# Retention and a gated feed-forward layer on one core: the state product padded to 128 rows, per-tile tables, and a new order of steps

## The chip, the cores and the metric

The kernel runs on one core of a Trainium2 chip. The metric is the device time of one execution in microseconds (us); a profiled execution gives the trace, whose span is a little shorter than that execution's time.

## The reference

Two layers follow each other. The first is a retention layer without softmax on `q`, `k`, `v` of shape (4, 8, 768, 64): batch, heads, tokens, head size.

```python
gamma = 1.0 - 2.0 ** (-5.0 - np.arange(H))
for t in range(S):
    state = gamma[None, :, None, None] * state + np.einsum('bhd,bhe->bhde', k[:, :, t], v[:, :, t])
    y[:, :, t] = scale * np.einsum('bhd,bhde->bhe', q[:, :, t], state)
```

Its result, 3072 tokens by 512, is the input `x` of the second layer, with weights of 512x1536, 512x1536 and 1536x512:

```python
gate = 1.0 / (1.0 + np.exp(-(x @ w_gate)))
val = x @ w_val
return (gate * val @ w_out).astype(np.float32)
```

All inputs and the output are float32; the kernel computes products in bfloat16 with float32 sums.

## The kernel before

**Tiles and pairs.** The 768 tokens are cut into six tiles t of 128 tokens. A pair P is one tile of two of the four batch elements, so P = 2t and 2t + 1 make a tile of all four: 512 columns of the second layer's input `xT`. Twelve pairs in all; tile t's feed-forward part runs while tile t + 1's retention part is prepared.

**Retention in chunks.** For a pair, q and k are transposed into `qkT` (two heads of 64 above each other on 128 partitions), by TensorE for pairs 0 to 3 (step T) and by DMA transposes that SyncE (SP) issues for the later ones (step J). `scores` multiplies k and q of a head (64 rows), `masks` multiplies the scores by a decay table on VectorE into `st`, `intra` multiplies v and `st` (128x64 stationary) into y, and before it `inter` adds the part of the earlier tiles: the running state times q, 64x64 per head, heads in two halves of the array. `state` multiplies the scaled k (`kt`) and v into the bank `z`, `state_sum` adds it to `za` on VectorE, and `state_out` scales `za` to the next tile's first token into `zq`, by ScalarE in four slices. `y_out` evicts y into `xT` on VectorE, times a table `taby`. The kernel keeps k scaled by gamma to the minus token, so one mask `maskd` (made from row 0 of `tabk`) and one `taby`, both relative to the tile, serve all tiles after the first.

**Feed-forward.** An up step (`up`, 128 of the 1536 hidden columns; `up_half` works on two such blocks and half of the tokens) makes four matmuls of 512 columns for the gate and four for the value into two banks, a sigmoid on ScalarE and a product on VectorE into `hT`. Tile 0 goes down by plain products (`down`). Tiles 1 to 5 use a seven-product scheme (`product` 1 to 7 of six matmuls of 256 columns, for two halves X and Y of the rows), with sums of hidden blocks on VectorE (`hidden_sums`, step S) and sums of weight blocks on GpSimd (POOL) with two casts on ScalarE (`weight_sums`, step W). `fast_out` evicts products 5, 6, 7 and 4 and stores finished rows from SP.

**Order.** Every engine runs its instructions in the order of the program. After a written prologue the program order is one string of steps per tile, `ORDER`; a minus sign means the tile before. Steps: u is `up`, a and b the two halves of `up_half`, d `down`, S and W the sums, X and Y products, L loads of a pair's k, q and v issued by POOL, H a tiny POOL copy that holds POOL until a pair's transposes have landed, J and T the transposes, k (VectorE) and m, n (ScalarE, four heads each) the scaling of k, O `state_out`, F the block of a new pair alone, E of a done pair alone, B of both.

```python
        "u1 u2 k0 u3 k1 u4 Z0 u5 u6 Z1 u7 u8 J4 J5 k2 T2 u9 F2 u10 u11",
```

A block in B runs inter (done), scores (new), intra (done), state (new) on TensorE, and y_out (done), masks (new), state_sum (new) on VectorE. All of PSUM's banks but one (the `z` bank) form one pool of seven that steps take in turn; a step waits until its bank has been read by its last reader.

**Transfers.** k, q, v and the weights come through POOL's queue (256 KB each for a pair's k, q and v); output rows and the DMA transposes are issued by SP.

Of the kernel before, what the change touches and what calls it, by code (L numbers as in the profile page):

```python
# [9 lines left out]
F32 = mybir.dt.float32  # L10
BF16 = mybir.dt.bfloat16
I32 = mybir.dt.int32
AX = mybir.ActivationFunctionType
ALU = mybir.AluOpType
# [3 lines left out]
def kernel(  # L18
# [10 lines left out]
    nc = tc.nc  # L29
    B, H, S, D = q.shape  # L30
    N_TOK, D_MODEL = out.shape
    D_FF = moe_w_gate.shape[1]
    C = 128
    NT = S // C
# [25 lines left out]
    def load(P, *what):  # L60
        for n in what:
            held, x = {"k": (kn, k), "q": (qn, q), "v": (vn, v)}[n]
            held[P] = ld.tile([C, 2 * H, D], BF16, tag=n, name=n + "n")
            nc.gpsimd.dma_start(out=held[P], in_=src(x, P))  # L64

    def load_one(P, c, *what):
        for n in what:
            held, x = {"k": (kn, k), "q": (qn, q), "v": (vn, v)}[n]
            if P not in held:
                held[P] = ld.tile([C, 2 * H, D], BF16, tag=n, name=n + "n")  # L70
            t, j = divmod(P, 2)
            nc.gpsimd.dma_start(out=heads(held[P], c),
                                in_=x[2 * j + c, :, t * C:(t + 1) * C, :].rearrange("h s d -> s h d"))
# [53 lines left out]
    for h in range(H):  # L127
        nc.scalar.activation(mask0[:, h % 2, h // 2, :], dist, AX.Exp, scale=lg[h], bias=lsc)
    maskd = const.tile([128, 2, NP, C], F32, name="maskd")
    tabk = const.tile([128, NT, H], F32, name="tabk")  # L130
    tabz = const.tile([128, NT, NP], F32, name="tabz")
    taby = const.tile([128, NP, C], F32, name="taby")

# [6 lines left out]
    def table_y():  # L140
        for p in range(NP):
            nc.scalar.activation(taby[:, p, :], toky, AX.Exp, scale=lgp[:, p:p + 1], bias=lsc)

    def table_mask():
        for i in range(2):
            nc.gpsimd.affine_select(maskd[:, i], tabk[:, 0, i:H:2].unsqueeze(2).to_broadcast([128, NP, C]),
                                    pattern=[[0, NP], [1, C]], base=0, channel_multiplier=-1,
                                    compare_op=ALU.is_ge, fill=0.0)

    qkT, kt, sc, st, y, zz, za, zq, xT = {}, {}, {}, {}, {}, {}, {}, {}, {}

# [22 lines left out]

    def scaled(P, part):
        x = kn[P].rearrange("s (c h) d -> s c h d", c=2)
        if part in (None, 0):
            kt[P] = ld.tile([C, 2 * H, D], BF16, tag="kt", name="kt", bufs=2)  # L180
        to = kt[P].rearrange("s (c h) d -> s c h d", c=2)
        if part is None:
            nc.vector.tensor_tensor(to, x, tabk[:, P // 2, :].unsqueeze(1).unsqueeze(3).to_broadcast([C, 2, H, D]),
                                    op=ALU.mult)
            return
        for h in range(part * NP, (part + 1) * NP):
            nc.scalar.activation(to[:, :, h, :], x[:, :, h, :], AX.Copy, scale=tabk[:, P // 2, h:h + 1])  # L187
# [9 lines left out]
    def masks(P, c):  # L197
        st[P, c] = []
        for i in range(2):
            s = at.tile([128, NP, C], BF16, tag="st", name="st", bufs=8)  # L200
            nc.vector.tensor_tensor(s, sc[P, c][i], (mask0 if P < 2 else maskd)[:, i], op=ALU.mult)  # L201
            st[P, c].append(s)

    def inter(P, c):
        y[P, c] = bank([128, NP, C])
        if P > 1:
            for p in range(NP):
                for i in range(2):
                    half = slice(i * D, (i + 1) * D)
                    nc.tensor.matmul(y[P, c][half, p, :], zq[P % 2][half, c, p, :], qkT[P][half, 1, c, p, :],  # L210
                                     start=(p == 0), stop=False, skip_group_check=True)
# [7 lines left out]
    def y_out(P, c, eng="a"):  # L219
        t = P // 2  # L220
        if t not in xT:
            xT[t] = at.tile([128, NP, 512], BF16, tag="xT", name="xT")
        col = (P % 2 * 2 + c) * C
        o = xT[t][:, :, col:col + C]
        if t == 0:
            (nc.scalar.copy if eng == "a" else nc.vector.tensor_copy)(o, y[P, c])  # L226
        else:
            nc.vector.tensor_tensor(o, y[P, c], taby, op=ALU.mult)  # L228

# [16 lines left out]
    def state_out(P):  # L246
        j = P % 2
        zq[j] = at.tile([128, 2, NP, D], BF16, tag=f"zq{j}", name="zq", bufs=1)
        for p in range(NP):
            nc.scalar.activation(zq[j][:, :, p, :], za[j][:, :, p, :], AX.Copy,  # L250
                                 scale=tabz[:, P // 2 + 1, p:p + 1])

    def has_state(P):
        return P is not None and P < NPAIR - 2

    def block(done, new):
        if done is not None:
            for c in range(2):
                inter(done, c)
        if new is not None:  # L260
            for c in range(2):
                scores(new, c)
        if done is not None:
            for c in range(2):
                intra(done, c)
        if has_state(new):
            state(new)
        if done is not None:
            for c in range(2):
                y_out(done, c)  # L270
        if new is not None:
            for c in range(2):
                masks(new, c)
        if has_state(new):
            state_sum(new)
# [4 lines left out]

    def up(t, n1, lo=0, hi=512):
        if t not in hT:
            hT[t] = ffn.tile([128, NFF, 512], BF16, tag="hT", name="hT", bufs=2)
        ps = []
        for w in (wg, wv):
            u = bank([128, 512])
            for kk in range(KT):
                nc.tensor.matmul(u[:, lo:hi], w[:, kk, n1 * 128:(n1 + 1) * 128], xT[t][:, kk, lo:hi],  # L288
                                 start=(kk == 0), stop=(kk == KT - 1))
            ps.append(u)  # L290
        gs = ffn.tile([128, 512], F32, tag="gs", name="gs")
        nc.scalar.activation(gs[:, lo:hi], ps[0][:, lo:hi], AX.Sigmoid)  # L292
        nc.vector.tensor_tensor(hT[t][:, n1, lo:hi], gs[:, lo:hi], ps[1][:, lo:hi], op=ALU.mult)  # L293

# [19 lines left out]
    def weight_sums(g, eng):  # L314
        fs = slice(2 * g, 2 * g + 2)
        b11, b12 = (wo2[:, fs, 0, c:c + 256] for c in (0, 256))
        b21, b22 = (wo2[:, fs, 1, c:c + 256] for c in (0, 256))
        t3 = ffn.tile([128, 2, 256], F32, tag="t3", name="t3", bufs=2)
        t2 = ffn.tile([128, 2, 256], F32, tag="t2", name="t2", bufs=2)
        eng.tensor_tensor(wt[:, 0, fs], b12, b11, op=ALU.subtract)  # L320
# [45 lines left out]
    def fast_out(t, i, n):  # L366
# [13 lines left out]
        if n == 7:  # L380
            nc.vector.tensor_tensor(hi[:, 256:], p5, a[:, :256], op=ALU.add)  # L381
        if n == 4:
            nc.scalar.copy(hi[:, :256], a[:, :256])
            nc.sync.dma_start(out=out[rows[1], :], in_=hi)

# [54 lines left out]
    transposes(1, 0, [0, 1], "a")  # L440
    table_y()
    keep_on(6)
    transposes(1, 1, [0, 1], "v", "v")
    scores(1, 0)
    scores(1, 1)
# [9 lines left out]
    for s in range(3, NFF // 2):  # L455
        load_gate_val(s)
    table_mask()
    load(2, "k", "q", "v")
    load(3, "k", "q", "v")
    for s in range(4):  # L460
        load_out(s)
    load(4, "k", "q", "v")
    load(5, "k", "q", "v")

    STEPS = {
        "u": lambda t, n: up(t, n),
        "a": lambda t, n: up_half(t, n, 0),
        "b": lambda t, n: up_half(t, n, 1),
# [8 lines left out]
        "T": lambda t, P: (new_qkT(P), transposes(P, 0, [0, 1], "a"), transposes(P, 1, [0, 1], "a")),  # L477
        "k": lambda t, P: scaled(P, None),
        "m": lambda t, P: scaled(P, 0),
# [3 lines left out]
        "B": lambda t, P: block(P - 1, P if P < NPAIR else None),  # L483
        "F": lambda t, P: block(None, P),
        "E": lambda t, P: block(P, None),
    }
    ORDER = [
        "u1 u2 k0 u3 k1 u4 Z0 u5 u6 Z1 u7 u8 J4 J5 k2 T2 u9 F2 u10 u11",
        "E2 k3 T3 a0 a2 F3 a4 a6 E3 O2 a8 W0 b0 O3 b2 W1 b4 b6 W2 m4 n4 a10 b8 H5 L6 L7 F4 b10 m5 -d0 n5 "
        "-d1 -d2 B5 J6 O4 -d3 S0 -d4 -d5 E5 J7 O5 -d6 S1 -d7 S2",  # L490
        "u0 -X1 -X2 u1 -X5 m6 u2 n6 -X3 -X6 u3 -X7 H7 L8 L9 u4 S0 -X4 F6 u5 m7 -Y1 -Y2 u6 n7 -Y5 u7 J8 "
        "-Y3 -Y6 u8 S1 J9 -Y7 u9 -Y4 B7 O6 u10 u11 E7 O7 S2",
        "-X1 -X2 u0 -X5 m8 u1 n8 -X3 -X6 u2 -X7 H9 L10 L11 u3 -X4 F8 u4 S0 m9 -Y1 -Y2 u5 n9 -Y5 u6 J10 "
        "-Y3 -Y6 u7 J11 -Y7 u8 S1 -Y4 B9 O8 u9 u10 E9 O9 u11 S2",
        "-X1 -X2 u0 -X5 u1 -X3 -X6 u2 -X7 u3 -X4 F10 u4 S0 -Y1 -Y2 u5 -Y5 u6 -Y3 -Y6 u7 -Y7 u8 S1 -Y4 B11 "
        "u9 u10 E11 u11 S2",
# [42 lines left out]
```

## Time and profile before

| | |
|---|---|
| time, median of three runs | 230.87 us (230.03 to 230.97) |
| the profiled execution's own time | 230.49 us |
| its span | 228.8 us |
| TensorE (PE) busy | 214.9 us, 94% |
| VectorE (DVE) busy | 139.8 us, 61% |
| ScalarE (ACT) busy | 102.8 us, 45% |
| GpSimd (POOL) busy | 70.4 us, 31% |
| moved by DMA | 25.22 MB, mean 110 GB/s |
| granted TensorE clock, mean | 0.989 |

In the page's slice lines a digit is the busy share of one of 40 slices of the span, in tenths (9 is 90% or more); a slice is 5.72 us. A timeline row gives the start, the time from the first start to the last end, the engine, the line of the kernel, the operation with output and inputs, the number of instructions merged into the row, and in brackets the idle time before it and what ended it. TensorE's matmuls are pipelined and their ends are modelled, so rows that follow each other overlap by some 0.16 us; and a few of its records are missing, which leaves a hole of one matmul in a row of otherwise even starts.

### The profile page before, as it was taken

How to read it: one execution, taken by the hardware profiler on the slowest of the kernel's cores; microseconds unless marked ns; L12 is line 12 of the kernel's file. 1: busy time of each engine (PE TensorE's matmuls, PEld its weight loads, DVE VectorE, ACT ScalarE, POOL GpSimd, SP SyncE). 2: the span in 40 equal slices, each digit the busy share in tenths (PEclk: the TensorE clock that was granted, in tenths of full speed). 3: DMA queues.
4: the chain of work that ended last, by engine and by line, in shares of the span. 5: the costliest groups of instructions: out<-in, count | busy, mean ns of one | idle time of the engine just before them, and what ended most of it. 6: DMA issues, size and time to landing. Idle time of an engine off the chain costs nothing.

```text
span 228.8 us, 4813 instructions
## 1 busy us (share of the span) xinstructions
PE 214.9 (94%) x1933; PEld 138.6 (61%) x1958; DVE 139.8 (61%) x266; ACT 102.8 (45%) x237; POOL 70.4 (31%) x77
## 2 busy tenths in 40 slices
PE   6668998999999999999999999999999999999992
PEld 6554444688885556566556565566566566664682
DVE  4763756876454973675693774983764974435630
ACT  7492465427776327273447362443233223323231
POOL 8978955699638001900092000000000000000000
PEclk9799999999999999999999999999999999999998
DMA  9999999999949999999999965200201101111013
GB/s 129 143 175 196 196 164 158 204 171 140 150 74 132 174 142 199 129 175 161 182 79 155 161 71 116 70 0 12 83 0 46 49 1 46 49 46 46 3 46 140
DMA packets 103703, 25.22 MB, mean 110 GB/s; under 512 B 93952, under 2 KB 100608, under 8 KB 103680
## 3 DMA queue, kind: packets, MB, share of 16 engines
q0 software_dynamic: 81248, 13.90, 79.7%
q1 hardware_dynamic: 22432, 11.01, 23.8%
q8 instruction: 15, 0.25, 0.5%
q14 instruction: 8, 0.07, 0.1%
HBM read 28.31 MB, written 6.29 MB: 151 GB/s over the span
## 4 chain that ended last, share of the span: by engine, by line
PE 77%; DMA 9%; POOL 6%; DVE 5%; issue 1%; ACT 0%; POOLq 0%; DVEq 0%
PE ff L288 36%; PE ff L363 19%; PE ff L304 9%; DMA qn<-in_q_dram 5%; PE ff L405 4%; DMA wv<-in_moe_w_val_dram 4%; PE ff L194 2%; PE ff L210 2%; PE ff L216 2%; DVE xT L228 2%; PE z L235 1%; DVE st L201 1%; POOL vn L64 1%; POOL kn L64 1%; POOL wg L85 1%
## 5 line engine op out<-in xcount | busy, mean ns | idle before, releaser
L293 DVE TENSOR_TENSOR hT<-gs,ff 128x512 bf16<-128x512 f32 (+1 forms) x61 | 41.1, 678 | 47.0 <-PE ff L288 39.6
L292 ACT ACTIVATE gs<-ff 128x512 f32<-128x512 f32 (+1 forms) x61 | 35.8, 589 | 63.5 <-PE ff L288 56.1
L288 PE MATMUL ff<-xT,wg 128*128 128x512 bf16 (+1 forms) x227 | 59.7, 376 | 2.9 <-DVE xT L226 1.1
L288 PE MATMUL ff<-xT,wv 128*128 128x512 bf16 (+1 forms) x239 | 61.2, 375 | 0.5
L288 PEld LDWEIGHTS <-wv 128*128 128x128 bf16 x244 | 23.9, 98 | 27.9
L288 PEld LDWEIGHTS <-wg 128*128 128x128 bf16 x244 | 22.7, 98 | 21.5 <-DVE xT L226 1.3
L363 PEld LDWEIGHTS <-hT 128*128 128x128 bf16 x240 | 23.4, 98 | 8.6 <-issue 1.0
L201 DVE TENSOR_TENSOR st<-ff,maskd 128x512 bf16<-128x512 f32 x40 | 24.8, 682 | 0.5 <-PE ff L194 0.4
L363 PEld LDWEIGHTS <-hs 128*128 128x128 bf16 x180 | 17.6, 98 | 5.4 <-issue 0.2
L363 PE MATMUL ff<-wt,hT 128*128 128x256 bf16 x120 | 16.0, 272 | 0.5 <-DVE ob L381 0.3
L363 PE MATMUL ff<-wt,hs 128*128 128x256 bf16 x120 | 16.2, 273 | 0.0
L228 DVE TENSOR_TENSOR xT<-ff,taby 128x512 bf16<-128x512 f32 x20 | 12.8, 684 | 5.2 <-PE ff L216 5.2
L250 ACT ACTIVATE zq<-za,tabz 128x128 bf16<-128x128 f32 x40 | 12.8, 390 | 6.6 <-PE ff L210 3.3
L187 ACT ACTIVATE kt<-kn,tabk 128x128 bf16<-128x128 bf16 x48 | 15.0, 390 | 0.0
L363 PE MATMUL ff<-wo,hT 128*128 128x256 bf16 x120 | 14.6, 273 | 0.1
L64 POOL DMA_DIRECT2D vn<-in_v_dram x12 | 14.0, 1169 | 1.7 <-DMA qn<-in_q_dram 0.6
L309 DVE TENSOR_TENSOR hT<-gs,ff 128x512 bf16<-128x512 f32 x12 | 8.1, 686 | 10.2 <-PE ff L304 7.3
L64 POOL DMA_DIRECT2D kn<-in_k_dram x11 | 12.8, 1165 | 2.7 <-DMA vn<-in_v_dram 1.3
L64 POOL DMA_DIRECT2D qn<-in_q_dram x11 | 12.7, 1158 | 1.4 <-PE ff L165 0.8
L304 PE MATMUL ff<-xT,wg 128*128 128x256 bf16 x96 | 12.5, 273 | 0.2 <-DVE xT L228 0.2
L304 PE MATMUL ff<-xT,wv 128*128 128x256 bf16 x96 | 12.4, 273 | 0.0
L417 POOL COPY kept<-qkT 128x2 bf16<-128x2 bf16 x3 | 0.6, 187 | 37.9 <-DMA qkT<-qn 37.9
(72 smaller groups left out, 242.5 us busy)
## 6 DMA issues: line engine op xcount, KB each, us to landing
out_dram<-ob SPq DMA_DIRECT2D x24, 256.0 KB, 2.3
vn<-in_v_dram POOLq DMA_DIRECT2D x12, 256.0 KB, 10.5
kn<-in_k_dram POOLq DMA_DIRECT2D x11, 256.0 KB, 8.1
qn<-in_q_dram POOLq DMA_DIRECT2D x11, 256.0 KB, 11.6
wo<-in_moe_w_out_dram POOLq DMA_DIRECT2D x4, 384.0 KB, 13.7
wg<-in_moe_w_gate_dram POOLq DMA_DIRECT2D x5, 256.0 KB, 9.2
wv<-in_moe_w_val_dram POOLq DMA_DIRECT2D x5, 256.0 KB, 9.1
raw<-in_k_dram SPq DMA_DIRECT2D x1, 256.0 KB, 3.4
```

The lines of the kernel that those rows point to most:

```text
L64: nc.gpsimd.dma_start(out=held[P], in_=src(x, P))
L187: nc.scalar.activation(to[:, :, h, :], x[:, :, h, :], AX.Copy, scale=tabk[:, P // 2, h:h + 1])
L201: nc.vector.tensor_tensor(s, sc[P, c][i], (mask0 if P < 2 else maskd)[:, i], op=ALU.mult)
L228: nc.vector.tensor_tensor(o, y[P, c], taby, op=ALU.mult)
L250: nc.scalar.activation(zq[j][:, :, p, :], za[j][:, :, p, :], AX.Copy, scale=tabz[:, P // 2 + 1, p:p + 1])
L288: nc.tensor.matmul(u[:, lo:hi], w[:, kk, n1 * 128:(n1 + 1) * 128], xT[t][:, kk, lo:hi], start=(kk == 0), stop=(kk == KT - 1))
L292: nc.scalar.activation(gs[:, lo:hi], ps[0][:, lo:hi], AX.Sigmoid)
L293: nc.vector.tensor_tensor(hT[t][:, n1, lo:hi], gs[:, lo:hi], ps[1][:, lo:hi], op=ALU.mult)
L304: nc.tensor.matmul(u[:, i], w[:, kk, (n1 + i) * 128:(n1 + i + 1) * 128], xT[t][:, kk, lo:lo + 256], start=(kk == 0), stop=(kk == KT - 1))
L309: nc.vector.tensor_tensor(hT[t][:, n1:n1 + 2, lo:lo + 256], gs, ps[1], op=ALU.mult)
L363: nc.tensor.matmul(to, left, right, start=(f == 0 and n in (1, 2)), stop=(f == NFF // 2 - 1), skip_group_check=True)
L405: nc.tensor.matmul(o, hT[t][:, n1, sm * 128:(sm + 1) * 128], wo[:, n1, :], start=(n1 == 0), stop=(n1 == NFF - 1))
```

## The change

- `inter` takes its stationary from `zbd`, one bfloat16 tile per pair of the tile with zeros off the diagonal blocks: 128 rows by 64 columns, and q of both heads as the moving side. The zeros are written once, by two memsets.
- `state_out` is two plain casts of `za`, one per half of the partitions. The decay that it applied moves into the tables: every tile has its own `maskd` and `taby`, made by POOL in `tile_tables` (step G, two affine selects and one product), tile 1's behind the loads of pairs 2 and 3, the others between the weight sums and between loads.
- A block runs scores (new), inter (done), intra (done), state (new), and on VectorE masks, y_out, state_sum.
- T2 stands behind u9, and F2 (as f, without its sum) behind u10; step p11 is u11 without its product, and that product (h) and the sum (V) follow E2. S1 stands before u8 or directly behind product 7. The slices n of the scaled k stand behind evictions.
- The table of y in the prologue stands behind the transposes of pair 1. k and q tiles have four buffers instead of five, t2 and t3 one instead of two.
- In the last tile the second row block of each half is stored in two halves, the very last half from ScalarE's queue.

The diff, shortened to its changed lines:

```diff
@@ -60,14 +60,14 @@
             held, x = {"k": (kn, k), "q": (qn, q), "v": (vn, v)}[n]
-            held[P] = ld.tile([C, 2 * H, D], BF16, tag=n, name=n + "n")
+            held[P] = ld.tile([C, 2 * H, D], BF16, tag=n, name=n + "n", bufs=5 if n == "v" else 4)
             nc.gpsimd.dma_start(out=held[P], in_=src(x, P))
...
             if P not in held:
-                held[P] = ld.tile([C, 2 * H, D], BF16, tag=n, name=n + "n")
+                held[P] = ld.tile([C, 2 * H, D], BF16, tag=n, name=n + "n", bufs=5 if n == "v" else 4)
             t, j = divmod(P, 2)
@@ -126,10 +126,13 @@
         nc.scalar.activation(mask0[:, h % 2, h // 2, :], dist, AX.Exp, scale=lg[h], bias=lsc)
-    maskd = const.tile([128, 2, NP, C], F32, name="maskd")
+    zbd = [const.tile([128, 2, NP, C], BF16, name=f"zbd{i}") for i in range(2)]
+    for z in zbd:
+        nc.vector.memset(z, 0.0)
     tabk = const.tile([128, NT, H], F32, name="tabk")
     tabz = const.tile([128, NT, NP], F32, name="tabz")
-    taby = const.tile([128, NP, C], F32, name="taby")
+    taby0 = const.tile([128, NP, C], F32, name="taby0")
+    maskd, taby = {}, {}
@@ -139,17 +142,20 @@
         for p in range(NP):
-            nc.scalar.activation(taby[:, p, :], toky, AX.Exp, scale=lgp[:, p:p + 1], bias=lsc)
-
-    def table_mask():
+            nc.scalar.activation(taby0[:, p, :], toky, AX.Exp, scale=lgp[:, p:p + 1], bias=lsc)
+
+    def tile_tables(t):
+        maskd[t] = at.tile([128, 2, NP, C], F32, tag="maskd", name="maskd")
         for i in range(2):
-            nc.gpsimd.affine_select(maskd[:, i], tabk[:, 0, i:H:2].unsqueeze(2).to_broadcast([128, NP, C]),
+            nc.gpsimd.affine_select(maskd[t][:, i], tabk[:, t, i:H:2].unsqueeze(2).to_broadcast([128, NP, C]),
                                     pattern=[[0, NP], [1, C]], base=0, channel_multiplier=-1,
                                     compare_op=ALU.is_ge, fill=0.0)
-
-
-
-    qkT, kt, sc, st, y, zz, za, zq, xT = {}, {}, {}, {}, {}, {}, {}, {}, {}
+        taby[t] = at.tile([128, NP, C], F32, tag="taby", name="taby")
+        nc.gpsimd.tensor_tensor(taby[t], taby0, tabz[:, t, :].unsqueeze(2).to_broadcast([128, NP, C]), op=ALU.mult)
+
+
+
+    qkT, kt, sc, st, y, zz, za, xT = {}, {}, {}, {}, {}, {}, {}, {}
@@ -174,14 +180,14 @@
-    def scaled(P, part):
+    def scaled(P, part, eng=None):
         x = kn[P].rearrange("s (c h) d -> s c h d", c=2)
...
         if part is None:
-            nc.vector.tensor_tensor(to, x, tabk[:, P // 2, :].unsqueeze(1).unsqueeze(3).to_broadcast([C, 2, H, D]),
-                                    op=ALU.mult)
+            eng.tensor_tensor(to, x, tabk[:, P // 2, :].unsqueeze(1).unsqueeze(3).to_broadcast([C, 2, H, D]),
+                              op=ALU.mult)
             return
@@ -198,7 +204,7 @@
             s = at.tile([128, NP, C], BF16, tag="st", name="st", bufs=8)
-            nc.vector.tensor_tensor(s, sc[P, c][i], (mask0 if P < 2 else maskd)[:, i], op=ALU.mult)
+            nc.vector.tensor_tensor(s, sc[P, c][i], (mask0 if P < 2 else maskd[P // 2])[:, i], op=ALU.mult)
             st[P, c].append(s)
@@ -207,7 +213,7 @@
                     half = slice(i * D, (i + 1) * D)
-                    nc.tensor.matmul(y[P, c][half, p, :], zq[P % 2][half, c, p, :], qkT[P][half, 1, c, p, :],
+                    nc.tensor.matmul(y[P, c][half, p, :], zbd[P % 2][:, c, p, half], qkT[P][:, 1, c, p, :],
                                      start=(p == 0), stop=False, skip_group_check=True)
@@ -225,7 +231,7 @@
         else:
-            nc.vector.tensor_tensor(o, y[P, c], taby, op=ALU.mult)
+            nc.vector.tensor_tensor(o, y[P, c], taby[t], op=ALU.mult)
@@ -245,40 +251,40 @@
         j = P % 2
-        zq[j] = at.tile([128, 2, NP, D], BF16, tag=f"zq{j}", name="zq", bufs=1)
-        for p in range(NP):
-            nc.scalar.activation(zq[j][:, :, p, :], za[j][:, :, p, :], AX.Copy,
-                                 scale=tabz[:, P // 2 + 1, p:p + 1])
+        for i in range(2):
+            half = slice(i * D, (i + 1) * D)
+            nc.scalar.copy(zbd[j][half, :, :, half], za[j][half])
...
-    def block(done, new):
-        if done is not None:
-            for c in range(2):
-                inter(done, c)
+    def block(done, new, sum_now=True):
         if new is not None:
...
             for c in range(2):
+                inter(done, c)
+            for c in range(2):
                 intra(done, c)
...
             state(new)
+        if new is not None:
+            for c in range(2):
+                masks(new, c)
         if done is not None:
...
                 y_out(done, c)
-        if new is not None:
-            for c in range(2):
-                masks(new, c)
-        if has_state(new):
+        if has_state(new) and sum_now:
             state_sum(new)
...
-    def up(t, n1, lo=0, hi=512):
+    gated = {}
+
+    def up(t, n1, lo=0, hi=512, finish=True):
         if t not in hT:
@@ -290,7 +296,13 @@
         nc.scalar.activation(gs[:, lo:hi], ps[0][:, lo:hi], AX.Sigmoid)
-        nc.vector.tensor_tensor(hT[t][:, n1, lo:hi], gs[:, lo:hi], ps[1][:, lo:hi], op=ALU.mult)
+        gated[t, n1] = (hT[t][:, n1, lo:hi], gs[:, lo:hi], ps[1][:, lo:hi])
+        if finish:
+            up_finish(t, n1)
+
+    def up_finish(t, n1):
+        to, gs, val = gated.pop((t, n1))
+        nc.vector.tensor_tensor(to, gs, val, op=ALU.mult)
@@ -315,8 +327,8 @@
         b21, b22 = (wo2[:, fs, 1, c:c + 256] for c in (0, 256))
-        t3 = ffn.tile([128, 2, 256], F32, tag="t3", name="t3", bufs=2)
-        t2 = ffn.tile([128, 2, 256], F32, tag="t2", name="t2", bufs=2)
+        t3 = ffn.tile([128, 2, 256], F32, tag="t3", name="t3", bufs=1)
+        t2 = ffn.tile([128, 2, 256], F32, tag="t2", name="t2", bufs=1)
         eng.tensor_tensor(wt[:, 0, fs], b12, b11, op=ALU.subtract)
@@ -379,9 +391,14 @@
             nc.vector.tensor_tensor(hi[:, 256:], p5, a[:, :256], op=ALU.add)
+            if t == NT - 1:
+                nc.sync.dma_start(out=out[rows[1], 256:], in_=hi[:, 256:])
         if n == 4:
             nc.scalar.copy(hi[:, :256], a[:, :256])
-            nc.sync.dma_start(out=out[rows[1], :], in_=hi)
+            if t == NT - 1:
+                (nc.scalar if i else nc.sync).dma_start(out=out[rows[1], :256], in_=hi[:, :256])
+            else:
+                nc.sync.dma_start(out=out[rows[1], :], in_=hi)
@@ -438,9 +455,9 @@
     transposes(1, 0, [0, 1], "a")
-    table_y()
     keep_on(6)
     transposes(1, 1, [0, 1], "v", "v")
+    table_y()
     scores(1, 0)
@@ -454,9 +471,9 @@
         load_gate_val(s)
-    table_mask()
     load(2, "k", "q", "v")
     load(3, "k", "q", "v")
+    tile_tables(1)
     for s in range(4):
@@ -464,6 +481,8 @@
         "u": lambda t, n: up(t, n),
+        "p": lambda t, n: up(t, n, finish=False),
+        "h": lambda t, n: up_finish(t, n),
         "a": lambda t, n: up_half(t, n, 0),
@@ -475,24 +494,28 @@
         "T": lambda t, P: (new_qkT(P), transposes(P, 0, [0, 1], "a"), transposes(P, 1, [0, 1], "a")),
-        "k": lambda t, P: scaled(P, None),
+        "G": lambda t, g: tile_tables(g),
+        "k": lambda t, P: scaled(P, None, nc.vector),
+        "K": lambda t, P: scaled(P, None, nc.gpsimd),
         "m": lambda t, P: scaled(P, 0),
...
         "F": lambda t, P: block(None, P),
+        "f": lambda t, P: block(None, P, False),
+        "V": lambda t, P: state_sum(P),
         "E": lambda t, P: block(P, None),
...
     ORDER = [
-        "u1 u2 k0 u3 k1 u4 Z0 u5 u6 Z1 u7 u8 J4 J5 k2 T2 u9 F2 u10 u11",
-        "E2 k3 T3 a0 a2 F3 a4 a6 E3 O2 a8 W0 b0 O3 b2 W1 b4 b6 W2 m4 n4 a10 b8 H5 L6 L7 F4 b10 m5 -d0 n5 "
-        "-d1 -d2 B5 J6 O4 -d3 S0 -d4 -d5 E5 J7 O5 -d6 S1 -d7 S2",
-        "u0 -X1 -X2 u1 -X5 m6 u2 n6 -X3 -X6 u3 -X7 H7 L8 L9 u4 S0 -X4 F6 u5 m7 -Y1 -Y2 u6 n7 -Y5 u7 J8 "
-        "-Y3 -Y6 u8 S1 J9 -Y7 u9 -Y4 B7 O6 u10 u11 E7 O7 S2",
-        "-X1 -X2 u0 -X5 m8 u1 n8 -X3 -X6 u2 -X7 H9 L10 L11 u3 -X4 F8 u4 S0 m9 -Y1 -Y2 u5 n9 -Y5 u6 J10 "
-        "-Y3 -Y6 u7 J11 -Y7 u8 S1 -Y4 B9 O8 u9 u10 E9 O9 u11 S2",
-        "-X1 -X2 u0 -X5 u1 -X3 -X6 u2 -X7 u3 -X4 F10 u4 S0 -Y1 -Y2 u5 -Y5 u6 -Y3 -Y6 u7 -Y7 u8 S1 -Y4 B11 "
+        "u1 u2 k0 u3 k1 u4 Z0 u5 u6 Z1 u7 u8 J4 J5 k2 u9 T2 u10 f2 p11",
+        "E2 -h11 V2 k3 T3 a0 a2 F3 a4 a6 E3 O2 a8 W0 b0 O3 G2 b2 W1 b4 m4 b6 W2 G3 n4 a10 b8 H5 L6 L7 F4 "
+        "m5 b10 n5 -d0 -d1 -d2 B5 J6 O4 -d3 S0 -d4 -d5 E5 J7 O5 -d6 S1 -d7 S2",
+        "u0 -X1 -X2 u1 -X5 m6 u2 -X3 -X6 n6 u3 -X7 H7 L8 G4 L9 u4 S0 -X4 F6 u5 m7 -Y1 -Y2 u6 -Y5 n7 u7 J8 "
+        "-Y3 -Y6 S1 u8 J9 -Y7 u9 -Y4 B7 O6 u10 u11 E7 O7 S2",
+        "-X1 -X2 u0 -X5 m8 u1 -X3 -X6 n8 u2 -X7 H9 L10 G5 L11 u3 -X4 F8 u4 S0 m9 -Y1 -Y2 u5 -Y5 n9 u6 J10 "
+        "-Y3 -Y6 u7 J11 -Y7 S1 u8 -Y4 B9 O8 u9 u10 E9 O9 u11 S2",
+        "-X1 -X2 u0 -X5 u1 -X3 -X6 u2 -X7 u3 -X4 F10 u4 S0 -Y1 -Y2 u5 -Y5 u6 -Y3 -Y6 u7 -Y7 S1 u8 -Y4 B11 "
         "u9 u10 E11 u11 S2",
```

## The prediction

> **What bounds the kernel now.** I read the page's busy times and slices first.
>
> ```profile
> PE 214.9 (94%) x1933; PEld 138.6 (61%) x1958; DVE 139.8 (61%) x266; ACT 102.8 (45%) x237; POOL 70.4 (31%) x77
> PE   6668998999999999999999999999999999999992
> DMA  9999999999949999999999965200201101111013
> ```
>
> TensorE (PE) is full from the fourth slice (17 us) to the last; up to there VectorE and ScalarE hand work to each other. DMA is full until slice 23 (131 us), so a load in that time lands when the queue gets to it, not when it is issued. What remains to be saved is what a PE-bound stretch loses between matmuls. The timeline of PE alone shows it, start to start, first at places without a named wait:
>
> ```profile
> 143.00 0.63 PE L210 MATMUL ff<-qkT,zq 64*64 64x128 bf16 x16
> 143.56 0.62 PE L194 MATMUL ff<-qkT 64*128 64x128 bf16 x16
> 144.11 0.64 PE L216 MATMUL ff<-st,vn 128*64 128x128 bf16 x16
> 144.58 0.42 PE L235 MATMUL z<-vn,kt 128*64 128x64 bf16 x16
> 144.93 1.04 PE L288 MATMUL ff<-xT,wg 128*128 128x512 bf16 x3
> ...
> 148.49 0.63 PE L210 MATMUL ff<-qkT,zq 64*64 64x128 bf16 x16
> 149.06 0.64 PE L216 MATMUL ff<-st,vn 128*64 128x128 bf16 x16
> ```
>
> Inter (L210) to scores (L194) is 0.56 us, scores to intra (L216) 0.55, but intra to state (L235), both 128*64, only 0.47 for the same 16 matmuls of 128 columns. Inter to intra in the lone block is 0.57. So a change of the array's shape (64*64, 64*128, 128*64) costs 0.09 to 0.10 us, and a group without one takes 0.47. Then the places with a wait, in the same timeline:
>
> ```profile
> 33.59 0.61 PE L165 MATMUL ff<-ident,kn 128*128 128x128 bf16 x8
> 35.16 0.62 PE L165 MATMUL ff<-ident,qn 128*128 128x128 bf16 x8 [0.97 <-DMA qn<-in_q_dram]
> ...
> 43.52 0.61 PE L165 MATMUL ff<-ident,qn 128*128 128x128 bf16 x8
> 44.28 1.03 PE L304 MATMUL ff<-xT,wg 128*128 128x256 bf16 x8 [0.16 <-DVE xT L228]
> ...
> 108.13 1.03 PE L288 MATMUL ff<-xT,wv 128*128 128x512 bf16 x4
> 109.42 0.81 PE L363 MATMUL ff<-wt,hT 128*128 128x256 bf16 x6 [0.26 <-DVE ob L381]
> ...
> 116.79 1.49 PE L363 MATMUL ff<-wo,hT 128*128 128x256 bf16 x12
> 118.46 1.04 PE L288 MATMUL ff<-xT,wg 128*128 128x512 bf16 x3 [0.19 <-DVE xT L228]
> ```
>
> The bracket counts idle time only after the modelled end of a matmul, so I take start to start less the usual pitch. Eight transposes usually take 0.46 (43.06 to 43.52): lost 1.57 - 0.46 = 1.11 for q of pair 2, and 0.76 - 0.46 = 0.30 at 44.28. Four 512-column matmuls take 0.865: lost 1.29 - 0.865 = 0.43 at 109.42. Twelve of 256 take 1.31: lost 1.67 - 1.31 = 0.36 at 118.46. Rows of three matmuls with a 0.2 us hole are lost records, not waits.
>
> **The change, part by part**, against the profiled execution's 230.49 us (span 228.8 and 1.7 around it; 0.38 under the median 230.87, inside the spread 230.03 to 230.97).
>
> *Inter as 128x64.* It costs no more per matmul if two column halves still run side by side: L210 and L216 both give 16 starts in 0.45 plus a switch, 28 ns each. The four blocks B (5, 7, 9, 11) go from inter, scores, intra, state to scores, inter, intra, state: three shapes become two. The six blocks E (2, 3, 5, 7, 9, 11) lose the step from inter to intra. Ten times 0.095 = **0.95 gained**. TensorEngine Tiling (Array Packing), Theoretical Speedup and Available Configurations, speaks against it: a contraction of 64 belongs in 64-row tiles, four of 64x64 against two of 128x64, so padding halves the packing; by that alone the 160 matmuls would take twice as long. The row decides: 28 ns shows that only two of the four tiles were in use.
>
> *T2 after u9; F2 after u10.* Up step u9 (1.73 us) now runs from 33.59 to 35.32, and q of pair 2 is wanted at 35.8. It landed by 35.16 and lands no earlier or later: the queue is full, so taking the mask (1.23 us on POOL) from in front of its issue moves nothing (bound: up to 1.2 earlier, already covered). **1.11 gained.** What is late next: scores of F2 need both evictions by ScalarE (1.01 each, from 35.95 to 37.9) and start at 38.05, a tie. Queued behind them on ScalarE is u10's sigmoid (to 38.5), then its product on VectorE (to 39.2), then four masks at 0.60 (to 41.65); intra of E2 would want the fourth at 41.55. Cost 0 to 0.5, I take 0.15. Moving u11's product (step h) and the state sum behind y_out keeps them off this chain; what they release (one bank, the sum for pair 4) is wanted 2 us later. The xT rows then end with T3's transposes, so of the 0.30 at 44.28 **0.15 is gained**. T3 comes up to 1.3 us sooner and needs q of pair 3: the fourth load after it was issued at 40.82 on that landing, T3's q part comes at about 42.5.
>
> *Masks before y_out in B; S1 before u8 (tile 2).* At 109.42 product 4 waited for the eviction of product 7, which stood on VectorE behind S1 (four of 0.34 pitch, 1.5 us with gaps). With S1 in front of u8 it fits under u8's matmuls: **0.43 gained**. From there VectorE ran without a gap to 118.4: y_out 1.21, masks 2.4, sum 0.6, two products 1.2, y_out 1.2, beginning only at 111.73, 1.66 us after product 4 ended. Masks need scores alone and may start 0.4 us after that end; I get the last y_out 0.3 us ahead of u0: **0.36 gained**. Bounds for the two together: 0 to 0.79. The k slices behind evictions move ScalarE's 1.27 us past 0.36 and 0.58 us copies; no PE wait stands there now, worth 0.
>
> *State copies.* Four scaled slices of 390 ns (1.27 for a group) become two casts of half the partitions; nearest row, the 128x512 cast L324, 610 ns, so 1.1: a ScalarE gain of 0.1 to 0.2 eight times, off the path: 0. They now wait for an inter that lies 0.55 later; the sigmoid behind had 1.06 of idle time in front (113.17), which covers it. Uncovered it would be 0.5 twice a tile.
>
> *Tables per tile.* POOL pays 1.23 for the masks and, by the 128x512 f32 row L322, 1.16 for y: 2.4 us five times, one 1.23 removed. Tile 1's stands before the wo loads, which waited up to 1.70 us for earlier landings anyhow: 0. G2 and G3 lie among the weight sums, now with one buffer each for t3 and t2: the sums end 2.4 us later (63.6), and the last ScalarE casts hold back n4 and two sigmoids, whose banks F4's scores at 65 want. Bounds 0 to 0.5, I take 0.1. G4 and G5 stand behind the holds of pairs 7 and 9 (to 90.1 and 114.0): loads 9 and 11 go 2.4 us later, transposes J9 and J11 on SP and the output rows queued behind J9 too; B9 wants pair 9 at 143, output buffers are four: 0. Whether these GpSimd operations and VectorE slow each other: beside the sums at 46 to 61 us the products took 686 ns, as elsewhere. But those have one operand in PSUM; hidden sums (418 ns, both in SBUF) never ran beside GpSimd arithmetic. Bounds 0 to 1 us of PE, I take 0.05, the row's side. SBUF — State Buffer, Who interferes with whom, is against the change here: a VectorE operation with two SBUF inputs and a GpSimd one that reads SBUF exclude each other for a whole instruction. By that rule S0 and G4 near 95 us would take turns; the sum would go to its upper bound.
>
> *Memsets.* Two of 512 elements before the first cast, where VectorE idles 0.85 for a load (4.26). Each between 0.06 (64x1 memset) and 0.54 (128x512 cast L428): cost 0 to 0.22, I take 0.05.
>
> *Last rows in halves.*
>
> ```profile
> 224.54 1.00 SPq L384 DMA_DIRECT2D out_dram<-ob x2
> 224.81 0.37 ACT L383 COPY ob<-ff 128x256 f32<-128x256 f32 x1 [0.30 <-PE ff L363]
> ```
>
> ```profile
> out_dram<-ob SPq DMA_DIRECT2D x24, 256.0 KB, 2.3
> ```
>
> The last store starts at 225.2 and takes 2.3; the other 1.3 is the end of the program. Half the bytes: at the page's best 196 GB/s 128 KB are 0.67 us, shared with the other store; at worst nothing, or 0.13 lost on a first issue (0.46 for the first on SP, 0.33 later). I take **0.2 gained**.
>
> Sum: 0.95 + 1.11 + 0.15 + 0.43 + 0.36 + 0.2 = 3.20 gained, less 0.15 + 0.1 + 0.05 + 0.05 = 0.35: 2.85. 230.49 - 2.85 = 227.64; 228.0 on the median's scale. I say 227.7; the likeliest case spans 226.8 to 228.6.
>
> **Rivals.** (1) VectorE and ScalarE take back what the order frees: F2's masks cost 0.5, the waits at 109 and 118 stay (0.79), F4 0.5. The terms above become 0.95 + 1.11 + 0.15 + 0.2 - 0.5 - 0.5 - 0.1 = 1.3: 229.2. For it: VectorE ran gap-free from 106.9 to 119.9. Against: both moves start its work earlier without adding any. With the SBUF clash at its 1 us on top, 230.2, no change. (2) Slower: the two halves of inter, which now share all rows and the same moving tile, do not run side by side. Then 56 instead of 28 ns for 160 matmuls, +4.5: 232.1. It decides from 46 ns on (2.85 / 160 = 18 more). Against: intra's halves share all rows and run at 28; for: there the moving tiles differ. (3) The shape switch is not saved, since the price belongs to new weights or another bank: 228.6. Against: intra to state also changes both.
>
> **How the numbers follow.** Forecast 0.58, (3) 0.08, (1) 0.20 of which 0.05 with the clash, (2) and unnamed losses of its size 0.14. About 0.5% (1.15 us) is what can be told from no change: faster below 229.7. Faster 0.58 + 0.08 + 0.13 = 0.79, same 0.09, slower 0.12. From 226.8 the range reaches to 229.8, past (1); the clash and (2) stay out.
>
> **What would show it.** Right: inter to intra at 0.47 in every block; no PE wait on qn near 35, none on ob or xT near 107 and 116; the last store landing in about 2.1. Wrong: inter over 0.8 per 16; hidden sums above 0.45 us or table operations above 1.3 near 95; PE waits on st (E2) or on a sigmoid's bank (F4).

## The result and the profile after

The changed kernel takes 228.03 us, median of seven runs (227.51 to 229.08); the kernel before, run beside it, 230.43 (230.03 to 231.01). The ratio is 0.990, 95% interval 0.987 to 0.993: 2.4 us faster. The profiled execution is the slowest of the seven, 229.08 us, so its trace shows 1.4 us less than before and not 2.4. One execution further down, 231.36 us at a granted clock of 0.970, is left out of its median and ratio.

The page after, span and busy times:

```profile
span 227.4 us, 4849 instructions
PE 215.7 (95%) x1958; PEld 138.6 (61%) x1958; DVE 143.3 (63%) x268; ACT 103.0 (45%) x217; POOL 80.7 (35%) x90
```

GpSimd has 10.3 us more, VectorE 3.5 us more, although VectorE's program gained only two memsets (1.0 together): something made others of its instructions longer. The timeline of TensorE after, at the places that the prediction named (inter is L216 now, scores L200, intra L222, transposes L171, products L375):

```profile
35.38 0.61 PE L171 MATMUL ff<-ident,kn 128*128 128x128 bf16 x8
35.83 0.61 PE L171 MATMUL ff<-ident,qn 128*128 128x128 bf16 x8
...
42.40 0.61 PE L171 MATMUL ff<-ident,qn 128*128 128x128 bf16 x8
43.16 1.03 PE L316 MATMUL ff<-xT,wg 128*128 128x256 bf16 x8 [0.16 <-DVE xT L234]
...
108.90 1.03 PE L294 MATMUL ff<-xT,wv 128*128 128x512 bf16 x4
109.76 0.82 PE L375 MATMUL ff<-wt,hT 128*128 128x256 bf16 x6
...
116.90 1.48 PE L375 MATMUL ff<-wo,hT 128*128 128x256 bf16 x12
118.22 1.03 PE L294 MATMUL ff<-xT,wg 128*128 128x512 bf16 x4
...
143.30 0.64 PE L216 MATMUL ff<-qkT,zbd 128*64 128x128 bf16 x16
143.77 0.61 PE L222 MATMUL ff<-st,vn 128*64 128x128 bf16 x16
```

The wait for q of pair 2 is gone (0.45 from k to q), and so are the waits at 109 and 118 (0.86 and 1.32, the plain pitch). Inter to intra is 0.47. The wait for xT after E2 is still there, 0.30. And two waits are new, in the same timeline:

```profile
64.62 0.45 PE L200 MATMUL ff<-qkT 64*128 64x128 bf16 x9
65.75 0.38 PE L200 MATMUL ff<-qkT 64*128 64x128 bf16 x7 [0.68 <-ACT gs L320]
...
97.60 0.82 PE L375 MATMUL ff<-wo,hT 128*128 128x256 bf16 x6
99.58 0.82 PE L375 MATMUL ff<-wo,hT 128*128 128x256 bf16 x6 [1.16 <-DVE st L207]
```

The first splits F4's scores: 1.13 us from row to row for nine matmuls of 28 ns, 0.87 lost. The second lies in front of product Y2: 1.98 us instead of the 0.655 of six matmuls (half of the 1.31 for twelve), 1.33 lost. Together 2.20 us. With the gains that the trace shows (0.95 by shapes, 1.11, 0.79 on VectorE, 0.70 after the last copy) that is 3.55 - 2.20 = 1.35, and the spans differ by 1.4.

What stands behind the second wait, the timeline of VectorE and GpSimd:

```profile
94.92 1.16 POOL L64 DMA_DIRECT2D qn<-in_q_dram  x1
95.06 0.86 DVE L349 TENSOR_TENSOR hs<-hT 128x512 bf16<-128x512 bf16 x1
95.96 0.74 DVE L350 TENSOR_TENSOR hs<-hs,hT 128x512 bf16<-128x512 bf16 x1
96.05 1.17 POOL L64 DMA_DIRECT2D vn<-in_v_dram  x1
96.62 1.54 DVE L351 TENSOR_TENSOR hT<-hT 128x512 bf16<-128x512 bf16 x1
97.19 1.46 POOL L150 TENSOR_SCALAR_AFFINE_SELECT maskd<-tabk 128x512 f32<-128x512 f32 x2
98.08 0.85 DVE L352 TENSOR_TENSOR hs<-hT,hs 128x512 bf16<-128x512 bf16 x1
98.62 1.20 POOL L154 TENSOR_TENSOR taby<-taby,tabz 128x512 f32<-128x512 f32 x1
98.85 2.47 DVE L207 TENSOR_TENSOR st<-ff,maskd 128x512 bf16<-128x512 f32 x4
```

The four hidden sums of S0 take 0.74 to 1.54 us instead of 0.42 each; the masks of F6 start 2.3 us late, and Y2 wants the second bank they free. Only the third and the fourth sum meet G4's tables, with 1.55 of the 2.31 us lost. The first two, 0.76 of it, ran before G4 began, beside load issues alone. Behind the first wait, the timeline of ScalarE:

```profile
62.19 0.62 ACT L336 CAST wt<-t 128x512 bf16<-128x512 f32 x1 [0.71 <-POOL t L333]
63.43 0.62 ACT L337 CAST wt<-t 128x512 bf16<-128x512 f32 x1 [0.62 <-POOL t L334]
63.95 1.27 ACT L193 ACTIVATE kt<-kn,tabk 128x128 bf16<-128x128 bf16 x4
65.13 1.05 ACT L320 ACTIVATE gs<-ff 128x512 f32<-128x512 f32 x2
```

ScalarE waits twice for GpSimd's weight sums, then does n4, and only then a10's sigmoid, whose bank F4's scores want.

### The profile page after: what moved, and what is told of

It reads as the page before. It is cut to its first block, busy times and chain, and to the rows that moved or that the text cites. A ratio compares the mean times of both kernels' runs of the same rounds, so it can differ in the third digit from the quotient of the medians.

```text
span 227.4 us, 4849 instructions
## 1 busy us (share of the span) xinstructions
PE 215.7 (95%) x1958; PEld 138.6 (61%) x1958; DVE 143.3 (63%) x268; ACT 103.0 (45%) x217; POOL 80.7 (35%) x90
## 4 chain that ended last, share of the span: by engine, by line
PE 81%; POOL 8%; DMA 3%; ACT 3%; DVE 2%; issue 1%; ACTq 0%; DVEq 0%; POOLq 0%
PE ff L294 46%; PE ff L375 20%; PE ff L422 5%; DMA qn<-in_q_dram 3%; PE ff L316 2%; PE ff L200 2%; PE ff L216 2%; PE ff L222 2%; POOL t L334 2%; POOL wt L332 2%; POOL t L333 1%; PE z L241 1%; PE ff L171 1%; DVE xT L234 1%; ACT L467 1%
## 5 line engine op out<-in xcount | busy, mean ns | idle before, releaser
L294 PE MATMUL ff<-xT,wg 128*128 128x512 bf16 (+1 forms) x244 | 61.9, 376 | 2.0 <-DVE xT L232 1.1
L375 PEld LDWEIGHTS <-hT 128*128 128x128 bf16 x240 | 23.4, 98 | 9.5 <-issue 1.8
L375 PEld LDWEIGHTS <-hs 128*128 128x128 bf16 x180 | 17.6, 98 | 5.4 <-issue 0.2
L375 PE MATMUL ff<-wt,hT 128*128 128x256 bf16 x120 | 16.1, 273 | 0.3 <-DVE ob L390 0.3
L375 PE MATMUL ff<-wt,hs 128*128 128x256 bf16 x120 | 16.2, 273 | 0.0
L256 ACT CAST zbd<-za 64x512 bf16<-64x512 f32 x20 | 12.3, 616 | 8.5 <-PE ff L216 5.0
L375 PE MATMUL ff<-wo,hT 128*128 128x256 bf16 x120 | 14.7, 273 | 1.2 <-DVE st L207 1.2
```

What stands on the lines that cost most here:

```text
L256: nc.scalar.copy(zbd[j][half, :, :, half], za[j][half])
L375: nc.tensor.matmul(to, left, right, start=(f == 0 and n in (1, 2)), stop=(f == NFF // 2 - 1), skip_group_check=True)
```

## The experiments

**The two new waits.** Theory: G4 beside the hidden sums makes one, G2 between the weight sums the other. Rivals: other work near 95 us slows the sums; the single buffers of t2 and t3 make the casts late. Three kernels and the changed one again ran on one chip (kernel before: 230.69).

The changed kernel, no edit:

> The changed kernel once more, for its spread and a second trace beside the next three. In the first trace two new waits of TensorE stood: 0.87 us in F4's scores (65.75, a sigmoid late on ScalarE) and 1.33 us before product Y2 (99.58, masks late on VectorE behind slow hidden sums, 0.74 to 1.54 us instead of 0.42). Theory: both are there in every run, so spans of 227.0 to 227.5. Rival: the second depends on when the loads land and so on when G4 meets the hidden sums; then some executions lack it and lie 1.0 to 1.6 us lower, as the times from 227.5 to 229.1 suggest.

Median 228.10 (226.78 to 228.80). Its trace (227.76 us) has the wait before Y2 at 0.82, with three sums at 0.74 to 1.47, and no wait in F4: there GpSimd issued pair 5's v at 46.05 and not 47.13, so the weight sums ended 1.05 us sooner. So the theory is wrong, and the rival is right that the waits vary: one of the two is missing here, the other is smaller, and the spans of the two traces differ by 1.4.

The two traces also say what the second wait takes. The sums lost 2.31 us in the first and 1.80 in the second, TensorE 1.33 and 0.82: both times 0.98 of the delay cost nothing. In both, two sums are slow beside load issues alone (0.75 us together, no wait by itself), and without that the sums would have ended before G4 began, at 97.19 and 96.59.

```diff
-"... H7 L8 G4 L9 u4 S0 ..."
+"... H7 L8 L9 G4 u4 S0 ..."
```

> The tables of tile 4 behind the loads of pair 9 (L8 L9 G4 instead of L8 G4 L9), so that they run on GpSimd after hidden sums S0 of tile 2. Theory, tables and hidden sums exclude each other: the four sums near 95 us go back to 0.42 us each, the wait before Y2 is gone, 1.0 to 1.5 us less in those executions that had it. Rival, the sums were slow from something else near 95 us (load issues or landings): they stay at 0.7 us or more and the wait stays at about 1.3 us.

Median 227.10 (226.65 to 228.24), 1.0 under the changed kernel beside it; ratio to before 0.984, 0.982 to 0.987 (the changed kernel: 0.988, 0.985 to 0.991, so the intervals overlap). Its timeline of VectorE, the last of the four sums:

```profile
95.54 0.42 DVE L352 TENSOR_TENSOR hs<-hT,hs 128x512 bf16<-128x512 bf16 x1
```

All four sums take 0.42 and Y1 and Y2 run through, twelve matmuls in one row of 1.47 from 96.94, though loads of pair 8 were being issued beside the sums. The wait before Y2 is also missing from every later trace with G4 behind L9. But the first two sums, which the edit does not reach, are fast here too, so this run alone does not say how much the tables did.

```diff
-"... O3 G2 b2 W1 b4 m4 b6 W2 G3 n4 a10 b8 H5 L6 L7 F4 ..."
+"... O3 b2 W1 b4 m4 b6 W2 G2 n4 a10 b8 H5 L6 L7 G3 F4 ..."
```

> The tables of tiles 2 and 3 behind the weight sums (W0 W1 W2 G2, and G3 behind the loads of pairs 6 and 7). Theory, the 2.3 us of G2 between W0 and W1 made ScalarE's casts late, and its sigmoid of a10 with them: the sigmoid comes 1.5 to 2.3 us sooner, the 0.87 us wait in F4's scores is gone, 0.7 to 0.9 us less. Rival, the single buffers of t3 and t2 made the casts late: the wait stays above 0.5 us, with GpSimd waiting on ScalarE's casts.

Median 227.51 (226.65 to 227.91), ratio 0.985, 0.983 to 0.987. F4's scores run through, with the sigmoid at 63.34 instead of 65.13 (64.08 in the second trace of the changed kernel). The rival's buffers are not nothing: without G2 between W0 and W1, GpSimd stands idle for 1.22 us until ScalarE's cast L336, before it starts the second sum of W1 (L333) at 54.49. So of G2's 2.2 us only about 1.0 is won. In the first trace GpSimd did not wait for a cast anywhere in the weight sums, and they were late by G2 and by its late start; the buffers did not make that wait. G2's place alone does not make it either, since the second trace of the changed kernel and that of the run with G4 moved, both with G2 in its old place, lack it too. And here G4 is in its old place and the wait before Y2 is missing: three sums took 0.42, one 0.85 beside a load issue, and G4 began at 97.13, after all of them.

Both edits together:

> Both moves together. Theory: the two waits are separate and add up, 2.0 us less than the changed kernel where it has both, near 226.3 to 226.8 us. Rival: removing one only moves the wait to the next late thing on VectorE, and the two together gain less than 1 us.

Median 226.71 (226.28 to 226.93), ratio 0.982, 0.980 to 0.984: 1.4 us under the changed kernel beside it (0.988, 0.985 to 0.991). Neither wait is in its trace. That two moves gain more than one is not shown: from the first transposes of pair 2 to the end of the span it is 225.4 - 35.64 = 189.8 us with G4 moved, 224.9 - 35.18 = 189.7 with G2 and G3 moved, 224.6 - 34.82 = 189.8 with both, against 192.0 and 190.6 in the changed kernel's two traces. The rest of the difference in span lies in the first 35 us, which the moves do not touch. The narrow spread is that of four executions; on another chip (below) six ran from 226.58 to 228.87. The experiments below that undo a part start from this version.

**What slows the hidden sums**, measured by itself in one execution of the kernel before, where GpSimd has nothing to do after 125 us:

```diff
+    def probe(t, n):
+        nc.gpsimd.tensor_copy(kept[:, 2:4], hT[t][:, n, :2])      # waits for the product in front of S0
+        if t == 3:   # four affine_select(spare[:, i], tabk...), as in tile_tables
+        if t == 4:   # two tensor_tensor(spare[:, 0], taby, tabz...)
+        if t == 5:   # two dma_start(out=spare3, in_=src(x, 0))
-"... F8 u4 S0 ..."   "... F10 u4 S0 ..."   "... u3 -X4 S0 ..."
+"... F8 u4 Q4 S0 ..."   "... F10 u4 Q4 S0 ..."   "... u3 Q3 -X4 S0 ..."
```

> The kernel before, with spare GpSimd work next to hidden sums S0 late in the kernel, where GpSimd is otherwise idle: in tile 3 four affine selects that read a table, in tile 4 two products of two tables, in tile 5 two load issues of 256 KB into a spare tile; each set waits for the product that stands in front of S0 on VectorE. Theory, GpSimd work that reads SBUF and hidden sums (two operands in SBUF) exclude each other: in tiles 3 and 4 the four sums take 0.7 to 1.5 us each instead of 0.42, or the GpSimd operations are longer than 0.65 and 1.16 us; in tile 5 they stay at 0.42. Rival, load issues do it, as some slow sums beside them suggest: tile 5's sums are slow (0.85) and those of tiles 3 and 4 are not.

Its timeline of GpSimd, then that of VectorE:

```profile
133.92 2.17 POOL L423 TENSOR_SCALAR_AFFINE_SELECT spare<-tabk 128x512 f32<-128x512 f32 x3
...
167.53 2.22 POOL L428 TENSOR_TENSOR spare<-taby,tabz 128x512 f32<-128x512 f32 x2
...
199.22 1.22 POOL L432 DMA_DIRECT2D spare<-in_k_dram  x1
```

```profile
134.75 0.85 DVE L339 TENSOR_TENSOR hT<-hT 128x512 bf16<-128x512 bf16 x1
...
167.56 1.29 DVE L338 TENSOR_TENSOR hs<-hs,hT 128x512 bf16<-128x512 bf16 x1
168.77 1.26 DVE L339 TENSOR_TENSOR hT<-hT 128x512 bf16<-128x512 bf16 x1
169.96 0.41 DVE L340 TENSOR_TENSOR hs<-hT,hs 128x512 bf16<-128x512 bf16 x1
...
199.27 0.42 DVE L338 TENSOR_TENSOR hs<-hs,hT 128x512 bf16<-128x512 bf16 x1
```

Beside an affine select a sum takes 0.85 to 0.87, beside a product of tables 1.26 to 1.29, beside a load issue 0.42 (one issue ran beside three sums; the second came later). The affine selects stretch too, from 0.63 to 0.81. So tables and sums do slow each other, and the theory holds.

The Trainium skill, SBUF — State Buffer, Who interferes with whom, states this: a VectorE operation with two SBUF inputs and a GpSimd operation that reads SBUF exclude each other for a whole instruction, while one with at most one SBUF input does not contend, outside two fast modes. The traces agree on which pairs clash: F6's four masks, with one operand in PSUM, took their usual 2.47 beside the product at 98.62. That the lock lasts a whole instruction no run shows: a sum lost 0.43 to 0.45 beside selects of 0.81, and 0.84 to 0.87 beside products of 1.04 to 1.10.

**The gains, undone one by one** in the version with both moves (226.71, ratio 0.980 to 0.984). These runs were on another chip, where that version was not run again; the kernel before took 230.85 there and 230.69 on the first. Inter on 64 rows in the new order:

```diff
-zbd[P % 2][:, c, p, half], qkT[P][:, 1, c, p, :]
+zbd[P % 2][half, c, p, half], qkT[P][half, 1, c, p, :]
```

> The version with both moves, but inter on 64 rows again (the diagonal block of zbd times one head's q), in the new order of a block. Theory, a change of the array's shape costs 0.095 us: inter to intra goes from 0.47 to 0.57 us in all ten blocks, 0.95 us more in all. Rival, the 0.10 that was lost before belongs to new weights or another bank: inter to intra stays at 0.47 and the time is the same.

227.91 (227.84 to 228.22), 1.2 more; ratio 0.988, 0.986 to 0.990. Its timeline:

```profile
146.53 0.64 PE L216 MATMUL ff<-qkT,zbd 64*64 64x128 bf16 x16
147.10 0.64 PE L222 MATMUL ff<-st,vn 128*64 128x128 bf16 x16
```

0.57 again (0.56 to 0.57 in all ten blocks), with the same intra and the same banks behind it: the price is that of the shape. The old order around pair 2:

```diff
-"... k2 u9 T2 u10 f2 p11", "E2 -h11 V2 k3 ..."
+"... k2 T2 u9 F2 u10 u11", "E2 k3 ..."
```

> The version with both moves, with the old order around pair 2 (T2 u9 F2 u10 u11, E2 with u11's product in front). Theory: TensorE waits again for q of pair 2 between the two groups of transposes, 1.0 to 1.2 us, and the whole is slower by that. Rival: since the loads now stand in front of the tables, q lands sooner and the wait is under 0.4 us.

227.99 (227.71 to 228.12), 1.3 more; ratio 0.988, 0.986 to 0.990.

```profile
33.57 0.61 PE L171 MATMUL ff<-ident,kn 128*128 128x128 bf16 x8
35.34 0.62 PE L171 MATMUL ff<-ident,qn 128*128 128x128 bf16 x8 [1.16 <-DMA qn<-in_q_dram]
```

The wait is 1.77 - 0.46 = 1.31, and q comes at 35.3 as it did before. Its load was issued at 23.32 instead of 23.53, hardly sooner although the mask no longer stands in front of it, so the run does not test what an earlier issue would do. VectorE's old order in B, and S1 of tile 2 behind u8:

```diff
+ y_out(done, c) in front of masks(new, c) in block
-"... -Y6 S1 u8 J9 -Y7 ..."
+"... -Y6 u8 S1 J9 -Y7 ..."
```

> The version with both moves, with y_out before masks in B again and S1 of tile 2 behind u8. Theory: the waits before product Y4 of tile 2 (0.43) and before u0 of the next tile (0.36) come back, 0.8 us more. Rival, the order of scores in front of inter has changed what VectorE waits for, so that one of the two or both stay away: 0 to 0.4 us more.

227.69 (227.54 to 228.13), 1.0 more; ratio 0.987, 0.985 to 0.989. Both waits are back, 1.29 - 0.865 = 0.43 and 1.85 - 1.31 = 0.54:

```profile
106.74 1.03 PE L294 MATMUL ff<-xT,wv 128*128 128x512 bf16 x4
108.03 0.82 PE L375 MATMUL ff<-wt,hT 128*128 128x256 bf16 x6 [0.26 <-DVE ob L393]
...
115.17 1.48 PE L375 MATMUL ff<-wo,hT 128*128 128x256 bf16 x12
117.02 1.04 PE L294 MATMUL ff<-xT,wg 128*128 128x512 bf16 x3 [0.37 <-DVE xT L234]
```

**The last rows.** Whole again:

```diff
-hi[:, 256:] stored behind product 7, hi[:, :256] behind product 4 (Y: from ScalarE)
+nc.sync.dma_start(out=out[rows[1], :], in_=hi)
```

> The version with both moves, with the last rows stored whole from SP, as before. From the last copy's start to the end of the span it was 3.98 us before and 3.28 after. Theory: 3.9 to 4.0 again, 0.6 to 0.7 us more, since the last store has twice the bytes and waits behind another on SP. Rival: the difference lies in the end of the program, not in the store, and stays within 0.2 us.

227.19 (227.04 to 227.34), 0.5 more; ratio 0.985, 0.983 to 0.987, which overlaps that of the version with both moves.

```profile
221.94 0.37 ACT L395 COPY ob<-ff 128x256 f32<-128x256 f32 x1 [0.30 <-PE ff L375]
```

From the last copy's start to the end of the span it is 225.6 - 221.94 = 3.66; in the changed kernel 227.4 - 224.09 = 3.3. That is between expectation and rival. With whole rows this tail varies, 3.66, 3.85 and 3.99 in the three traces that have them (this one, the probe, the kernel before); with halves it is 3.2 to 3.3 in all ten. So halving is worth 0.4 to 0.7. Halves, but all from SP:

```diff
-(nc.scalar if i else nc.sync).dma_start(out=out[rows[1], :256], in_=hi[:, :256])
+nc.sync.dma_start(out=out[rows[1], :256], in_=hi[:, :256])
```

> The version with both moves, with the last rows in halves but all stores issued by SP. Theory, the bytes matter and not the queue: within 0.1 us of the version with both moves (last copy to end of span 3.3). Rival, ScalarE's own queue is what saves it, since SP is still busy with the store before: 0.2 to 0.4 us more, as with whole rows (3.66).

> The version with both moves once more, on the same chip as the one with all stores from SP: 226.3 to 227.0 us, ratio to the kernel before 0.980 to 0.984.

On this chip 226.78 with ScalarE's queue (ratio 0.985, 0.981 to 0.988) and 226.94 without (five executions; 0.987, 0.983 to 0.992): the intervals overlap and the times do not settle it. The version with both moves came within its expected time, its ratio a little above the expected one. The traces settle the queue: 224.5 - 221.28 = 3.2 from SP alone. The bytes matter, not the queue.

**The parts against the whole.** The traces can be compared without the first 35 us, which vary by about 1 us between traces of the same prologue: the span, less the start of pair 2's first transposes (where these stand in front of u9, less its 1.73 too).

| trace | span less start | more than both moves |
|---|---|---|
| both moves, two traces | 189.8, 189.8 | |
| inter on 64 rows | 226.1 - 35.21 = 190.9 | 1.1 |
| old order around pair 2 | 226.4 - 35.30 = 191.1 | 1.3 |
| VectorE's old order | 226.2 - 35.09 = 191.1 | 1.3, of which 0.35 a wait for q at 35.9 |
| whole rows | 225.6 - 35.46 = 190.1 | 0.3 to 0.4 |
| kernel before | 228.8 - 35.32 = 193.5 | 3.7 |

The four parts, 1.1 + 1.3 + 1.0 + 0.35, make 3.75, and all of them together 3.7: the four explain the gain of the version with both moves.

## Why the prediction was right, and where its sizes were off

- **Shapes, 0.95:** right. All ten blocks show 0.47; undone it costs 1.2 us by the medians and 1.1 by the traces. The rival that the halves would not run side by side fell: 16 matmuls in 0.45 us plus the step to the next group, 28 ns each. So did the rival of new weights or another bank.
- **Pair 2, 1.11:** right, 1.3 when undone. That the load is bound by the queue and not by its issue stays open: q was issued at 24.10 in the first trace, later than the 23.53 before, since GpSimd waited there for weights to land, where the mask had stood. And q does not always land by 35.16: it held TensorE for 0.35 at 35.90 in one trace of the new order. F2's masks cost about 0.07 of the 0.15 (E2's intra spans 0.62 instead of 0.55). The 0.15 at 43 did not come: TensorE still loses 0.30 behind T3, since y_out now waits for intra (0.25 idle) and not for VectorE's queue.
- **VectorE's order, 0.79:** right, both waits gone, 1.0 when undone.
- **Last rows, 0.2:** too small; 0.4 to 0.7 by the traces. Its rate of 196 GB/s is not the page's best, which is 204, and makes no difference (0.64 us for 0.67).
- **Weight sums, 0.1 (0 to 0.5):** 0.87 in the first trace, over the upper bound, and 0 in the second. The path was the one named (GpSimd, the casts, n4, a10's sigmoid, F4's bank), and the sums' end at 63.6 is that of the second trace. What was missed is that GpSimd's own start moves by 1 us between executions while TensorE came 1.1 us earlier.
- **GpSimd against VectorE, 0.05 (0 to 1):** the weakest step. The row chosen, products at 686 ns beside the weight sums, has one operand in PSUM and could not bear on sums with two in SBUF. The prediction said that these never ran beside GpSimd arithmetic, quoted the rule, named G4 and S0 near 95 us, and still took the row's side: TensorE waited 1.33 and 0.82 us in two traces, over the upper bound once. The rule alone does not give that number either, since in both the sums met G4 only after being slowed beside load issues, which neither the row nor the rule foresaw.
- **State copies at 0, memsets at 0.05:** right. Two casts take 1.24 instead of 1.27; the two memsets (0.49 each) fit into VectorE's idle time in front of the first cast, which starts at 4.19 instead of 4.26.

By its own signs the prediction was right only in part: all those of "right" came (the last store landed in 1.8 us, sooner than its 2.1), but so did two of "wrong", the slow sums and tables near 95 (two selects in 1.46 instead of 1.23) and the wait on F4's sigmoid. The total is right with some luck. Gains of 3.20 were expected and about 3.7 came, losses of 0.35 were expected and about 1.3 came (228.03 against 226.71 without the two waits): 2.85 expected, 2.4 by the medians. Of what rival (1) lists, F4's wait and the clash came, F2's masks cost 0.07 instead of 0.5, and the waits at 109 and 118 went. Its argument had a misreading: VectorE did not run gap-free from 106.9 to 119.9, it stood idle for 1.77 us in front of 111.73, as the prediction's own sum says.

## What to carry to other kernels

When a new operation is set beside an old one, look for a row with the same places of the operands, not only the same engines; if there is none, keep both ends of the bound in the sum. GpSimd tables belong where VectorE reads PSUM, or where nothing waits for the sums: in the version with both moves G3's product still stretches a sum at 75.8 us to 1.14, and TensorE does not wait. A step is put on GpSimd's queue after what ScalarE waits for there. A small matmul group can be padded with zeros to the shape of its neighbours for nothing when, as here, it used only two of the array's parts at a time (28 ns per matmul both ways).

## What the runs showed of the hardware

- A VectorE sum of two SBUF tiles (128x512 bf16, 0.42 us) becomes 0.85 to 0.87 beside a GpSimd affine select and 1.26 to 1.29 beside a GpSimd product; beside the load issue of the probe it stays at 0.42. Most sums beside load issues take 0.42 in the other traces too, but some take 0.74 to 0.86: three in the first trace of the changed kernel (the first two of S0 and L352 at 119.1), two in its second, one with G2 and G3 moved, three with both moved. Why is open.
- A change of the array's shape between groups of small matmuls costs 0.08 to 0.10 us here, for 64*64, 64*128 and 128*64.
- A ScalarE cast of 64 partitions by 512 takes 616 ns, as long as one of 128 partitions (610 to 620).
